# Chunk 1's x^T of a fused attention and MLP kernel: from token order and PE transposes to products in transposed order

## The chip, the cores and the metric

The kernel runs on one core of one Trainium2 chip. A core has five engines that take their instructions from queues of their own: TensorE (PE: matrix products and transposes), VectorE (DVE), ScalarE (ACT), GpSimd (POOL) and SyncE (SP, which issues most DMA transfers). They wait for each other through semaphores. SBUF is the working memory, 128 partitions wide; PSUM holds what PE writes, in banks of 512 fp32 words per partition. The metric is the device time of one execution in microseconds (us); lower is better.

## The reference: what is computed

Two blocks follow each other. The first is an attention with polynomial sketches, without softmax: 4 batches, 4 heads, 1088 tokens, head size 32, sketch size r = 8, so 64 features.

```python
def phi(x):
    a = np.einsum('rd,bhsd->bhsr', S1, x)
    b = np.einsum('rd,bhsd->bhsr', S2, x)
    return np.einsum('bhsi,bhsj->bhsij', a, b).reshape(*x.shape[:-1], r * r)
q_p, k_p = (phi(q), phi(k))
kv = np.einsum('bhsf,bhsd->bhfd', k_p, v)
z = np.sum(k_p, axis=2)
num = np.einsum('bhsf,bhfd->bhsd', q_p, kv)
den = np.einsum('bhsf,bhf->bhs', q_p, z)[..., None] + 1e-06
attn = num / den
```

The heads are laid side by side to x, 4352 tokens by 128. The second block is an MLP: `h = x @ w_in` (128 to 2048), exact GELU, `g @ w_out` (2048 to 128). w_in, w_out, S1 and S2 are 64-bit floats: they arrive as pairs of 32-bit words and are turned into fp32 on the chip.

## The kernel before, in words

**Chunks.** The tokens of each batch are cut into two chunks of 512, and what is left over (64 tokens of each batch) makes a ninth chunk. x is held transposed, x^T: 128 features on the partitions, 512 tokens along the free axis. For a chunk n and each of the 16 blocks fi of 128 hidden units, `hidden(n, fi)` is one matmul of w_in's block with xT[n], and a GELU by ACT; `project(n, fi)` adds w_out's block times that GELU to an output bank. Later chunks use a scheme with fewer products (`two_products`), which the change does not touch. `first_hidden` is hidden (n, 0) in halves of 256 tokens, so that it can begin when half of x^T is there.

**The beginning.** Chunks 0 and 1 are both of batch 0, and the MLP can't start before batch 0's kv and z are summed (`kv_first`, into kv_bank, copied by ACT to `kz[0]`). kz[0] holds, for two pairs of heads on the two halves of the partitions, kv (32 columns) and z (1 column). For chunks 0 and 1 `expand_products` makes the 64 features' two factors from q^T with 16 matmuls into two pairs of banks; `expand_copy` (ACT) copies one factor of each pair of banks to the tile A_sb, and `expand_multiply` (DVE) multiplies it with the other into qp (tile q_pT).

**x^T of chunks 0 and 1.** `numerators_by_token` makes numerator and denominator with tokens on the partitions: 32 matmuls of 33 columns. `divide` inverts the denominators and multiplies, on DVE. The result x_tok has tokens on the partitions, so PE transposes it in 128x128 pieces and ACT and DVE copy them into xT (`turn_half`, `turn_half_apart`).

**Weights.** w_in and w_out come in five pieces each (256, 256, 512, 512, 512 hidden units). The class `Rounding` turns a piece into fp32: low words and exponents on ACT, fields (exponent and mantissa fields), mantissas and signs on DVE, the product on DVE or POOL; for w_out's second piece the mantissas go through a copy by ACT (tile bits_high) and an addition on POOL (`by_pool=True`). w_in's second piece serves hidden blocks 2 and 3, w_out's second piece projections 2 and 3.

**What sets the order.** Nothing plans it: the order of the text is the order in each engine's queue, and the last lines of the kernel fix it so. The beginning is written out; from there a loop over steps t runs. Steps t = 0 to 3 are hidden (0,0) to (0,3) with w_out's first two pieces beside them; in step 3 chunk 1's numerators, division and turns stand between the first projections. Step 4 does chunk 1's first hidden, then alternates hidden and projection. PSUM has two banks each for hidden and output and two pairs of work banks.

Of the kernel before, what the change touches and what calls it, by code (L numbers as in the profile page):

```python
# [16 lines left out]
def kernel(  # L17
# [29 lines left out]
    JC = 4  # L47
    CW = JC * 128
    G = 128 // 32
    NCH = J // JC  # L50
# [26 lines left out]
    def hidden_bank():  # L77
        return hps.tile([128, CW], FP, name="h_ps")

# [149 lines left out]

    kz_first = big.tile([128, 128], FP, name="kz_first")  # L230

# [257 lines left out]
    def sketch_of_z(b, ps, at):  # L489
# [6 lines left out]
                       in1=own_r[:, None, :, None].broadcast_to([128, 2, 2, 4]))  # L496

    def repeat_first_z():

        of = kz[0].rearrange("f (r x) -> f r x", r=2)  # L500
        to = kz_first.rearrange("f (c r d) -> f c r d", c=NP, r=2)
        for c in range(NP):
            act.copy(out=to[:F, c], in_=of[c * F:(c + 1) * F, :, 0:D])
        zs = att.tile([128, 2, D], FP, name="z_cols")
        pool.tensor_copy(out=zs, in_=of[:, :, D:C].broadcast_to([128, 2, D]))
        held["zs"] = zs
# [26 lines left out]
    def expand_products(n):  # L533


        W = width[n]
        for i in range(2):
            B_of[n, i] = work_banks()
        for s in range(2):
            for g in range(G):  # L540
                for c in range(NP):
                    rows = slice(g * D, (g + 1) * D)
                    pe.matmul(B_of[n, g // 2][c * F:(c + 1) * F, g % 2, s * W // 2:(s + 1) * W // 2],  # L543
                              lhsT=Srep[rows, s].rearrange("p i j -> p (i j)"),
                              rhs=qT[n][rows, 2 * c:2 * c + 2].rearrange("p r j t -> p r (j t)"), start=True, stop=True)
        qp[n] = att.tile([128, 2, CW], FP, name="q_pT")
# [5 lines left out]
    def expand_multiply(n, i):  # L552
        W = width[n]
        a, b = (t.rearrange("f g (r x) -> f g r x", r=2) for t in (A[i][:, :, :W // 2], B_of[n, i][:, :, W // 2:W]))
        dve.tensor_mul(out=qp[n].rearrange("f r (g x) -> f g r x", g=G)[:, 2 * i:2 * i + 2], in0=a, in1=b)

# [64 lines left out]
    def attend_products(n, banks=None):  # L621
# [7 lines left out]
        for i in range(m):  # L629
            for s in range(2):  # L630
                rows, b = slice(s * 64, (s + 1) * 64), batch_of(n, s, i)
                for h in range(H):
                    pe.matmul(banks[h * D:(h + 1) * D, s, i * N:(i + 1) * N],  # L633
                              lhsT=(kz[b] if b else kz_first)[rows, h * D:(h + 1) * D],
                              rhs=f[rows, h // 2, i, :, h % 2], start=True, stop=True)
        numerators_in[n] = banks

    def take_x(n):
# [4 lines left out]
        to = to.rearrange("p (s x) -> p s x", s=2) if m == 1 else to.rearrange("p (s t i) -> p s i t", s=2, i=m)  # L643
        act.copy(out=to, in_=banks[:, :, :W // 2] if m == 1 else banks[:, :, :W // 2].rearrange("p s (i t) -> p s i t", i=m))  # L644

    x_tok = {}
# [95 lines left out]
    T = {}  # L742
    HW = CW // 2
    NPAIR = NF // 2
# [184 lines left out]
    kz_of, kv_of = (x.rearrange("f (r x) -> f r x", r=2)[:, :, :C] for x in (kz[0], kv_bank[:, :128]))  # L929
    act.copy(out=kz_of, in_=kv_of)  # L930
    w_in[0].mantissas()
    w_in[0].signs()
    w_in[0].product(pool)
    load_w_out(0, gated=True)
    load_rest()
    w_out = [Rounding(w, beside=b) for w, b in zip(w_out_sb[:2], w_in)]
    by_act(**late[0])
    w_in[1].low_words()
    parts = [range(2), range(2, JC)]
    nd = [[hidden_bank(), hidden_bank()], [out_bank(), out_bank()]]  # L940
    for banks, tokens in zip(nd, parts):
        numerators_by_token(0, banks, tokens)
    den = denominators(nd[1])
    expand_products(1)
    divide(0, nd[0], parts[0], by_head_pair=True)
    w_in[1].exponent_fields()
    w_in[1].exponents()
    divide(0, nd[1], parts[1], by_head_pair=True, den=den)
    turn_half(0, 0, hidden_bank(), by_act)
    w_in[1].mantissa_fields()  # L950
    turn_half_apart(0, 1, [out_bank(), out_bank()])
    w_in[1].mantissas()
    w_in[1].signs()
    w_in[1].product()
    for half in range(2):
        first_hidden(0, half)
    for i in range(2):
        expand_copy(1, i)
    for i in range(2):
# [204 lines left out]
    for t in range(len(steps) + LAG):  # L1164
        if t < 4:
# [7 lines left out]
            if t == 2:  # L1173
                w_out[1].low_words()
            if t == 3:
                banks = work_banks()
                numerators_by_token(1, halves(banks), range(JC))
                w_out[1].mantissas(by_pool=True)
                w_out[1].exponents()
                divide(1, banks, range(JC), by_head_pair=False)  # L1180
                w_out[1].signs()
                w_out[1].product()
                project(0, 0)
                project(0, 1, cols=slice(0, 256))
                turn_half(1, 0, work_bank(), by_act)
                project(0, 1, cols=slice(256, 512))
                turn_half(1, 1, work_bank(), by_dve)
            continue
        if t == 4:
            first_hidden(1, 0)  # L1190
            for f, *a in products[t]:
                f(*a)
            first_hidden(1, 1)
        for n in drains[t]:
# [60 lines left out]
```

## Time and profile before

| | us |
|---|---|
| median of 3 runs | 259.5 (259.48 to 259.85) |
| span of the profiled execution, first to last instruction | 258.0 |
| PE busy | 253.9 (98% of the span) |
| DVE / ACT / POOL busy | 151.0 / 115.5 / 163.5 |
| numerators of chunk 1 on PE (L656) | 19.11 to 20.25 |
| hidden (1,1) begins on PE (L721) | 24.24 |

The profile gives no total of its own for the profiled execution beside its span; the span is 1.5 us under the median of the runs. A line of a timeline or a group names source line, engine, operation, output<-input by the program's tile names, and a count. PE works as two records per fp32 matmul. Busy time says little on an engine off the critical path; what counts here is the order of events between 12 and 25 us and what each instruction waited for. Lines in the profile are those of the kernel before.

### The profile page before, as it was taken

What the parts mean: (1) busy time and instruction counts of PE and PEld (TensorE: products, weight loads), DVE (VectorE), ACT (ScalarE), POOL (GpSimd) and SP (SyncE); (2) the same over time, 40 slices, a digit from 0 to 9 for tenths busy, and PEclk for the clock granted to TensorE, in tenths of its full rate; (3) what the DMA queues carried; (4) which work ended last, traced back from release to release, by engine and by line L of the source; (5) the groups of instructions that cost most, each with busy time, mean ns of one, the idle gap of its engine ahead of it and who ended that gap; (6) DMA issues with size and microseconds to landing.
All of it is one profiled execution on the core that took longest, in us unless ns stands there. A gap on an engine that the chain in (4) does not pass through costs nothing.

```text
span 258.0 us, 5769 instructions
## 1 busy us (share of the span) xinstructions
PE 253.9 (98%) x2335; PEld 136.1 (53%) x2335; DVE 151.0 (59%) x312; ACT 115.5 (45%) x224; POOL 163.5 (63%) x173
## 2 busy tenths in 40 slices
PE   8999999999999999999999999999999999999995
PEld 7856444345444545544444455455444444445794
DVE  2786888969699997590187986399307000700330
ACT  4685777443626332443335332533444334433442
POOL 3403006799968788487758775787758777877300
PEclk9999999999999999999999999999999999999999
DMA  6469848721000101102000002000200200020020
GB/s 199 144 185 374 188 95 217 213 76 14 3 0 12 31 1 21 23 6 37 3 0 3 0 9 38 0 1 3 41 3 4 39 0 1 7 36 0 3 41 20
DMA packets 29594, 13.48 MB, mean 52 GB/s; under 512 B 21888, under 2 KB 27776, under 8 KB 29568
## 3 DMA queue, kind: packets, MB, share of 16 engines
q1 hardware_dynamic: 29392, 13.05, 20.3%
q8 instruction: 18, 0.29, 0.5%
q10 hardware_dynamic: 176, 0.07, 0.1%
q14 instruction: 8, 0.07, 0.1%
HBM read 10.88 MB, written 2.23 MB: 51 GB/s over the span
## 4 chain that ended last, share of the span: by engine, by line
PE 98%; DVE 1%; issue 0%; ACT 0%; DVEq 0%
PE h_ps L721 45%; PE o_ps L807 33%; PE o_ps L858 5%; PE w_ps L855 3%; PE w_ps L437 1%; PE w_ps L890 1%; PE w_ps L578 1%; PE w_ps L633 1%; PE o_ps L426 1%; PE h_ps L737 1%; PE w_ps L978 1%; PE w_ps L656 0%; PE w_ps L543 0%; DVE x_tok L679 0%; PE h_ps L333 0%; PE w_ps L333 0%
## 5 line engine op out<-in xcount | busy, mean ns | idle before, releaser
L721 PE MATMUL h_ps<-xT,w_in 128*64 128x512 f32 (+3 forms) x514 | 136.9, 576 | 0.0
L728 ACT ACTIVATE block<-h_ps 128x512 f32<-128x512 f32 (+1 forms) x128 | 73.0, 571 | 117.3 <-PE h_ps L721 115.3
L721 PEld LDWEIGHTS h_ps<-xT,w_in 128*64 128x64 f32 (+1 forms) x514 | 41.9, 143 | 30.4 <-issue 11.6
L807 PE MATMUL o_ps<-block,w_out 128*64 128x256 f32 x224 | 57.5, 379 | 0.0
L772 POOL TENSOR_TENSOR bits_low<-block 128x512 f32<-128x512 f32 x28 | 35.9, 1281 | 27.8 <-ACT block L728 27.8
L807 PEld LDWEIGHTS o_ps<-block,w_out 128*64 128x64 f32 x224 | 30.5, 137 | 38.0 <-issue 27.5
L773 POOL TENSOR_TENSOR bits_a<-block 128x512 f32<-128x512 f32 x28 | 35.7, 1277 | 12.0 <-ACT block L728 11.9
L822 DVE COPY sums<-o_ps 64x256 f32<-64x256 f32 x8 | 3.3, 416 | 60.6 <-PE o_ps L807 60.6
L774 POOL TENSOR_TENSOR bits_e<-bits_a,block 128x512 f32<-128x512 f32 x28 | 36.0, 1286 | 2.2
L775 POOL TENSOR_TENSOR bits_m<-block,bits_e 128x512 f32<-128x512 f32 x28 | 35.8, 1279 | 2.2
L807 PE MATMUL o_ps<-bits_low,small 128*64 128x256 f32 x112 | 28.8, 380 | 0.0
L807 PE MATMUL o_ps<-bits_a,small 128*64 128x256 f32 x112 | 28.8, 380 | 0.0
L807 PE MATMUL o_ps<-block,small 128*64 128x256 f32 x112 | 28.8, 379 | 0.0
L807 PE MATMUL o_ps<-bits_m,w_out 128*64 128x256 f32 x112 | 28.8, 380 | 0.0
L807 PEld LDWEIGHTS o_ps<-block,small 128*64 128x64 f32 x112 | 15.2, 137 | 17.9 <-issue 10.8
L807 PE MATMUL o_ps<-bits_e,small 128*64 128x256 f32 x112 | 17.1, 383 | 0.0
L858 PE MATMUL o_ps<-g,w_out 128*128 128x512 f32 (+1 forms) x34 | 16.5, 572 | 0.0
L807 PEld LDWEIGHTS o_ps<-bits_m,w_out 128*64 128x64 f32 x112 | 15.4, 137 | 0.0
L807 PEld LDWEIGHTS o_ps<-bits_a,small 128*64 128x64 f32 x112 | 15.2, 137 | 0.0
L807 PEld LDWEIGHTS o_ps<-bits_low,small 128*64 128x64 f32 x112 | 15.2, 137 | 0.0
L590 DVE STREAM_TRANSPOSE w_ps<-w_ps 128x512 f32<-128x512 f32 (+1 forms) x7 | 4.8, 687 | 17.1 <-ACT xT L644 12.7
L807 PEld LDWEIGHTS o_ps<-bits_e,small 128*64 128x64 f32 x112 | 7.7, 137 | 10.6 <-issue 8.8
(194 smaller groups left out, 305.1 us busy)
## 6 DMA issues: line engine op xcount, KB each, us to landing
block<-in_moe_w_in_dram SPq DMA_DIRECT2D x3, 512.0 KB, 8.4
block<-in_moe_w_out_dram SPq DMA_DIRECT2D x3, 512.0 KB, 12.1
k<-in_k_dram SPq DMA_DIRECT2D x12, 128.0 KB, 3.1
v<-in_v_dram SPq DMA_DIRECT2D x12, 128.0 KB, 3.4
q<-in_q_dram SPq DMA_DIRECT2D x24, 64.0 KB, 2.4
out_dram<-oT SPq DMA_DIRECT2D x21, 64.0 KB, 2.2
k<-in_k_dram SPq DMA_DIRECT2D x2, 256.0 KB, 2.8
q<-in_q_dram SPq DMA_DIRECT2D x2, 256.0 KB, 3.9
```

The costliest lines, as they stand in the source:

```text
L426: pe.matmul(ps[c * F:(c + 1) * F, r * 2 * D:r * 2 * D + C], lhsT=flat(k_p[0, r][:, t, c * 4 + ch * 2 + one]), rhs=v_aug[r][:, c, i, :C], s ...
L590: dve.transpose(out=tok, in_=ps[:, :, :H2])
L721: pe.matmul(ps[rows, :W], lhsT=w[:, rows], rhs=xT[n][:, :W], start=True, stop=True)
L728: act.activation(out=g_of[n, fi][:, :W], in_=ps[:, :W], func=ACT.Gelu)
L772: pool.tensor_sub(out=s[3], in0=a11, in1=a21)
L773: pool.tensor_add(out=s[1], in0=a21, in1=a22)
L774: pool.tensor_sub(out=s[2], in0=s[1], in1=a11)
L775: pool.tensor_sub(out=s[4], in0=a12, in1=s[2])
L807: pe.matmul(acc[n][bank][half * 64:(half + 1) * 64, col:col + HW], lhsT=fixed, rhs=moving, start=opens and e == 0 and name in "4715", stop ...
L822: dve.tensor_copy(out=N[lo, 0, one], in_=a0[lo, one])
L855: pe.matmul(o_of[n][i][:, :128], lhsT=g[:, i * 128:(i + 1) * 128], rhs=w_tile(w_out_sb, fi), start=first, stop=final)
L858: pe.matmul(o_of[n][:, cols], lhsT=w_tile(w_out_sb, fi), rhs=g[:, cols], start=first, stop=final)
```

## The change

x^T of chunk 1 is made without turning x back by PE. ACT spreads kz[0] into `kz_both`, which holds all four heads' kv and z on each half of the partitions (four copies of 64x66, right behind the copy of kz[0]); POOL repeats z 32 times per head (`z_wide`). The features of chunk 1 are laid so that each half of the partitions holds all heads of half of the tokens. `ratio_products` then makes, with 16 matmuls of 32 output rows and 256 columns, the denominators repeated over 32 rows and the numerators, both already transposed. `ratio_inverse` turns the repeated denominators in 32x32 blocks on DVE, takes one column of each, adds 1e-6 and inverts; `ratio` turns them back, repeated, and multiplies the numerators into xT[1], in two halves.

In the order: the products stand in step 2, ahead of the hidden block of step 3; the inverse and the multiplications stand beside w_out's second piece in step 3; projections (0,0) and (0,1) are no longer interleaved with turns, and chunk 1's first hidden now follows projection (0,2). w_in's second piece: both fields on DVE ahead of chunk 0's divisions, exponents on ACT ahead of the copies of chunk 0's x^T, mantissas and signs behind the divisions, the product on POOL. The first A_sb copy of chunk 1 moves on ACT ahead of these exponents, the second behind the copies of chunk 0's x^T. `kz_first`, which the ninth chunk used, is replaced by kz_both.

```diff
--- before.py
+++ after.py
@@ -46,6 +46,7 @@
     REM = S - MAIN
     JC = 4
     CW = JC * 128
+    HW = CW // 2
     G = 128 // 32
     NCH = J // JC
     C = D + 1
@@ -227,7 +228,8 @@
 
     kz = [big.tile([128, 128], FP, name=f"kz{b}") for b in range(B)]
 
-    kz_first = big.tile([128, 128], FP, name="kz_first")
+    kz_both = big.tile([128, H, 2 * D], FP, name="kz_both")
+    z_wide = big.tile([128, H, D], FP, name="z_wide")
 
     ones = big.tile([128, D], FP, name="ones")
 
@@ -495,12 +497,19 @@
         dve.tensor_mul(out=S_abc[b][:, :, :, 4:8], in0=c.rearrange("p (i f) -> p i f", i=2)[:, :, None].broadcast_to([128, 2, 2, 4]),
                        in1=own_r[:, None, :, None].broadcast_to([128, 2, 2, 4]))
 
+    def spread_first_kv():
+
+        of = kz[0].rearrange("f (r x) -> f r x", r=2)
+        for s in range(2):
+            for c in range(NP):
+                act.copy(out=kz_both[s * F:(s + 1) * F, 2 * c:2 * c + 2, :C], in_=of[c * F:(c + 1) * F, :, :C])
+
+    def spread_first_z():
+        pool.tensor_copy(out=z_wide, in_=kz_both[:, :, D:C].broadcast_to([128, H, D]))
+
     def repeat_first_z():
 
         of = kz[0].rearrange("f (r x) -> f r x", r=2)
-        to = kz_first.rearrange("f (c r d) -> f c r d", c=NP, r=2)
-        for c in range(NP):
-            act.copy(out=to[:F, c], in_=of[c * F:(c + 1) * F, :, 0:D])
         zs = att.tile([128, 2, D], FP, name="z_cols")
         pool.tensor_copy(out=zs, in_=of[:, :, D:C].broadcast_to([128, 2, D]))
         held["zs"] = zs
@@ -542,7 +551,8 @@
                     rows = slice(g * D, (g + 1) * D)
                     pe.matmul(B_of[n, g // 2][c * F:(c + 1) * F, g % 2, s * W // 2:(s + 1) * W // 2],
                               lhsT=Srep[rows, s].rearrange("p i j -> p (i j)"),
-                              rhs=qT[n][rows, 2 * c:2 * c + 2].rearrange("p r j t -> p r (j t)"), start=True, stop=True)
+                              rhs=(qT[n][rows, :, 2 * c:2 * c + 2] if n else qT[n][rows, 2 * c:2 * c + 2])
+                              .rearrange("p r j t -> p r (j t)"), start=True, stop=True)
         qp[n] = att.tile([128, 2, CW], FP, name="q_pT")
 
     def expand_copy(n, i):
@@ -551,6 +561,10 @@
 
     def expand_multiply(n, i):
         W = width[n]
+        if n:
+            dve.tensor_mul(out=qp[n].rearrange("f r (g x) -> f (r g) x", g=2)[:, 2 * i:2 * i + 2],
+                           in0=A[i][:, :, :W // 2], in1=B_of[n, i][:, :, W // 2:W])
+            return
         a, b = (t.rearrange("f g (r x) -> f g r x", r=2) for t in (A[i][:, :, :W // 2], B_of[n, i][:, :, W // 2:W]))
         dve.tensor_mul(out=qp[n].rearrange("f r (g x) -> f g r x", g=G)[:, 2 * i:2 * i + 2], in0=a, in1=b)
 
@@ -631,7 +645,7 @@
                 rows, b = slice(s * 64, (s + 1) * 64), batch_of(n, s, i)
                 for h in range(H):
                     pe.matmul(banks[h * D:(h + 1) * D, s, i * N:(i + 1) * N],
-                              lhsT=(kz[b] if b else kz_first)[rows, h * D:(h + 1) * D],
+                              lhsT=kz[b][rows, h * D:(h + 1) * D] if b else kz_both[rows, h, :D],
                               rhs=f[rows, h // 2, i, :, h % 2], start=True, stop=True)
         numerators_in[n] = banks
 
@@ -642,6 +656,36 @@
         to = xT[n][:, :W]
         to = to.rearrange("p (s x) -> p s x", s=2) if m == 1 else to.rearrange("p (s t i) -> p s i t", s=2, i=m)
         act.copy(out=to, in_=banks[:, :, :W // 2] if m == 1 else banks[:, :, :W // 2].rearrange("p s (i t) -> p s i t", i=m))
+
+    def ratio_products(n, banks):
+
+        f = qp[n].rearrange("f r (g h t) -> f h (r g) t", g=2, h=H)
+        for at, w in ((HW, lambda rows, h: z_wide[rows, h]), (0, lambda rows, h: kz_both[rows, h, :D])):
+            for s in range(2):
+                rows = slice(s * F, (s + 1) * F)
+                for h in range(H):
+                    pe.matmul(banks[h * D:(h + 1) * D, s, at:at + HW], lhsT=w(rows, h), rhs=f[rows, h], start=True, stop=True)
+
+    def ratio_inverse(banks):
+
+        turned = att.tile([128, 2 * CW], FP, name="q_f", bufs=1)
+        dve.transpose(out=turned[:, :CW].rearrange("p (g s x) -> p s g x", g=G, s=2),
+                      in_=banks[:, :, HW:].rearrange("p s (g x) -> p s g x", g=G))
+        den = att.tile([128, NP, JC * 2], FP, name="den_tok").rearrange("p c k -> p (c k)")
+        dve.tensor_scalar(out=den, in0=turned[:, :CW].rearrange("p (k x) -> p k x", x=D)[:, :, 0], scalar1=1e-6, scalar2=None,
+                          op0=AX.add)
+        dve.reciprocal(out=den, in_=den)
+        return den, turned[:, CW:]
+
+    def ratio(n, banks, den, wide):
+
+        xT[n] = att.tile([128, CW], FP, name="xT", bufs=3)
+        for i in range(2):
+            cols = slice(i * HW, (i + 1) * HW)
+            dve.transpose(out=wide[:, cols], in_=den[:, i * 8:(i + 1) * 8, None].broadcast_to([128, 8, D]))
+            by = lambda t: t.rearrange("p (g s x) -> p s g x", g=2, s=2)
+            dve.tensor_mul(out=by(xT[n][:, cols]), in0=banks[:, :, i * 128:(i + 1) * 128].rearrange("p s (g x) -> p s g x", g=2),
+                           in1=by(wide[:, cols]))
 
     x_tok = {}
 
@@ -740,7 +784,6 @@
 
     blocks, sums, acc = {}, {}, {}
     T = {}
-    HW = CW // 2
     NPAIR = NF // 2
 
     PLACE = {"1": (0, 0, 0), "2": (0, 0, HW), "3": (1, 0, 0), "5": (1, 0, HW),
@@ -928,34 +971,35 @@
     query_turn(1, lambda **a: late.append(a))
     kz_of, kv_of = (x.rearrange("f (r x) -> f r x", r=2)[:, :, :C] for x in (kz[0], kv_bank[:, :128]))
     act.copy(out=kz_of, in_=kv_of)
+    spread_first_kv()
     w_in[0].mantissas()
     w_in[0].signs()
     w_in[0].product(pool)
     load_w_out(0, gated=True)
     load_rest()
+    spread_first_z()
     w_out = [Rounding(w, beside=b) for w, b in zip(w_out_sb[:2], w_in)]
     by_act(**late[0])
     w_in[1].low_words()
+    w_in[1].fields()
     parts = [range(2), range(2, JC)]
     nd = [[hidden_bank(), hidden_bank()], [out_bank(), out_bank()]]
     for banks, tokens in zip(nd, parts):
         numerators_by_token(0, banks, tokens)
     den = denominators(nd[1])
     expand_products(1)
+    expand_copy(1, 0)
+    w_in[1].exponents()
     divide(0, nd[0], parts[0], by_head_pair=True)
-    w_in[1].exponent_fields()
-    w_in[1].exponents()
     divide(0, nd[1], parts[1], by_head_pair=True, den=den)
-    turn_half(0, 0, hidden_bank(), by_act)
-    w_in[1].mantissa_fields()
-    turn_half_apart(0, 1, [out_bank(), out_bank()])
     w_in[1].mantissas()
     w_in[1].signs()
-    w_in[1].product()
+    w_in[1].product(pool)
+    turn_half(0, 0, hidden_bank(), by_act)
+    turn_half_apart(0, 1, [out_bank(), out_bank()])
     for half in range(2):
         first_hidden(0, half)
-    for i in range(2):
-        expand_copy(1, i)
+    expand_copy(1, 1)
     for i in range(2):
         expand_multiply(1, i)
     w_out[0].fields()
@@ -1172,24 +1216,23 @@
                 w_out[1].fields()
             if t == 2:
                 w_out[1].low_words()
+            if t == 2:
+                banks = work_banks()
+                ratio_products(1, banks)
             if t == 3:
-                banks = work_banks()
-                numerators_by_token(1, halves(banks), range(JC))
                 w_out[1].mantissas(by_pool=True)
                 w_out[1].exponents()
-                divide(1, banks, range(JC), by_head_pair=False)
+                inverse = ratio_inverse(banks)
                 w_out[1].signs()
                 w_out[1].product()
+                ratio(1, banks, *inverse)
                 project(0, 0)
-                project(0, 1, cols=slice(0, 256))
-                turn_half(1, 0, work_bank(), by_act)
-                project(0, 1, cols=slice(256, 512))
-                turn_half(1, 1, work_bank(), by_dve)
+                project(0, 1)
             continue
         if t == 4:
-            first_hidden(1, 0)
             for f, *a in products[t]:
                 f(*a)
+            first_hidden(1, 0)
             first_hidden(1, 1)
         for n in drains[t]:
             drain(n)
```

## The prediction

> **What bounds the kernel now.** I read the page first, for the bound.
>
> ```profile
> PE 253.9 (98%) x2335; PEld 136.1 (53%) x2335; DVE 151.0 (59%) x312; ACT 115.5 (45%) x224; POOL 163.5 (63%) x173
> PEclk9999999999999999999999999999999999999999
> PE 98%; DVE 1%; issue 0%; ACT 0%; DVEq 0%
> ```
>
> TensorE (PE) is busy throughout at full clock, and the chain that ended last is PE from 15.04 us to the end: there the list of waits has no PE wait over the 0.2 us before L694. So whatever PE gains or loses before about 25 us moves the end by as much. The change lies between 12 and 25 us; hence the timeline there, PE first (start, duration, engine, line).
>
> ```profile
> 7.71 1.12 PE L543 MATMUL w_ps<-qT,Srep 32*64 32x256 f32 x32
> 13.34 1.12 PE L543 MATMUL w_ps<-qT,Srep 32*64 32x256 f32 x32
> 14.39 0.44 PE L702 MATMUL h_ps<-ident,x_tok 128*128 128x128 f32 x2
> 15.04 0.41 PE L694 MATMUL o_ps<-ident,x_tok 128*128 128x128 f32 x2 [0.21 <-DVE x_tok L679]
> 15.38 1.13 PE L737 MATMUL h_ps<-xT,w_in 128*128 128x128 f32 x8
> 16.35 2.84 PE L721 MATMUL h_ps<-xT,w_in 128*128 128x512 f32 x6
> 19.11 1.14 PE L656 MATMUL w_ps<-kz,q_pT 64*64 64x33 f32 x64
> 20.18 1.56 PE L858 MATMUL o_ps<-g,w_out 128*128 128x512 f32 x4
> 24.24 1.02 PE L721 MATMUL h_ps<-xT,w_in 128*128 128x512 f32 x2
> 68.99 0.64 PE L633 MATMUL w_ps<-q_pT,kz 64*32 64x256 f32 x16
> ```
>
> A matmul is two records, and a 512-column one takes 0.86 us of PE (pairs start that far apart). At 24.24 starts hidden(1,1), by which projections (0,0) to (0,2), hidden (0,0) to (0,3) and chunk 1's first hidden are done; after the change the same work is done when hidden(1,1) starts. I measure the change by that start. Then ScalarE (ACT), which has the copies:
>
> ```profile
> 7.38 0.33 ACT L398 COPY a_t<-o_ps 128x64 f32<-128x64 f32 x2 [0.43 <-PE o_ps L382]
> 8.87 1.07 ACT L550 COPY A_sb<-w_ps 128x512 f32<-128x512 f32 x2 [0.60 <-PE w_ps L543]
> 12.38 0.59 ACT L937 COPY qT<-w_ps 128x512 f32<-128x512 f32 x1 [0.34 <-PE w_ps L333]
> 12.86 0.44 ACT L260 ACTIVATE bits_low<-small 128x256 f32<-128x256 uint32 x1
> 14.28 0.51 ACT L279 ACTIVATE bits_r<-bits_e,below 128x256 uint32<-128x256 uint32 x1 [0.58 <-DVE bits_e L268]
> 14.86 0.37 ACT L703 COPY xT<-h_ps 128x256 f32<-128x256 f32 x1
> 19.62 0.58 ACT L728 ACTIVATE g<-h_ps 128x512 f32<-128x512 f32 x1
> 20.27 0.42 ACT L284 ACTIVATE bits_high<-bits_a 128x256 f32<-128x256 uint32 x1
> 20.60 0.49 ACT L279 ACTIVATE bits_r<-bits_e,below 128x256 uint32<-128x256 uint32 x1
> 22.13 0.45 DVE L297 TENSOR_TENSOR w_out<-bits_m,bits_e 128x256 f32<-128x256 f32 x1
> 85.87 0.49 ACT L503 COPY kz_first<-kz 64x64 f32<-64x64 f32 x2
> ```
>
> Three things to see. The A_sb copy of chunk 0 (8.87) began 0.04 us after the last record of its products (7.71+1.12 = 8.83), although it needs only the first of the two bank pairs. Two small copies out of PSUM (7.38) overlap: 0.33 us for two of 0.22, so 0.11 apart. Two SBUF-to-SBUF copies that change partition halves (85.87) do not: 0.49 for two, 0.24 apart. And bits_high, the first step of w_out's second piece, follows gelu (0,3) at 19.62 in ACT's queue.
>
> **The change, part by part** (waits as the two built programs order them; engines take their queues in order).
>
> *1. Four spread copies ahead of the qT copy.* They follow the kz copy (11.84 to 12.04) on ACT, each 64x66 SBUF to SBUF, alternating partition halves. Unknown price: 0.11 apart (L398) or 0.24 (L503). I take 0.24: same engine, same memories, same alternation. Then they run from 12.07 to 13.05, and the qT copy that took 12.38 to 12.97 takes 13.06 to 13.65. Chunk 1's products (L543, 13.34) wait for it: hand-over 0.06, start 13.71, late by 0.37. At 0.11 apart qT ends at 13.10 and nothing is late. Ends: 0 and 0.37.
>
> *2. A_sb copy and exponents now stand ahead of chunk 0's xT copy on ACT.* By the 8.87 row the A_sb copy starts 0.04 after the last product: 13.71+1.12+0.04 = 14.87. The next ACT starts follow 0.48 (half of the L550 pair's start distance) and 0.42 later (18.40 to 18.81 in the same view): exponents 15.35, xT copy 15.77, to 16.14 at 0.37. first_hidden starts 0.06 later, 16.20, where L737 started at 15.38: **+0.82** with step 1's 0.37 inside. Its bounds: 0.45 if step 1 costs nothing; 0.22 less if the A_sb copy waited only for the third quarter of the products. The DVE step taken out between the divisions (L268, 0.20) would have let PE transposes start 0.20 earlier; ACT's copy is later, so it is worth 0.
>
> *3. w_in's second piece.* Its fields go before the first division: DVE idles 0.54 before 12.99 and two such steps start 0.20 apart, so they fit; its load landed long before 12.46, as ACT read it freely at 12.86. Mantissas and signs follow the divisions, signs end at 16.32 (exponents end 15.86, plus 0.04 and 0.42); the product on POOL takes 0.73 (the first piece's), 16.40 to 17.13. hidden(0,2) needs it at 17.21+0.82 = 18.03: hidden by 0.9, and z_wide ahead of it on POOL too (0.23 for 128x64 to 0.61 for 128x512, from about 13.3). That cover is gone only if signs slip past 17.2. No transfer is moved; SP's queue is as before, and the gating memsets on POOL still come before z_wide.
>
> *4. PE work.* Removed: the 32 numerators of L656 (19.02, when hidden(0,3)'s last record gives way, to 20.18: 1.16, and 0.10 of exposed weights behind), four transposes (0.11 each, 0.44) and 0.08 of weights: 1.78. Added: 16 matmuls of the form of L633, eight of which take 0.43; with the 0.10 and 0.14 that this timeline shows on entering and leaving such tiles, and 0.09 of exposed weights behind: 1.21 (0.88 of it the matmuls). Net **-0.57**. If only four of the eight tiles ran at once, 0.88 more.
>
> *5. hidden(0,3) moves behind the products, and gelu (0,3) with it; bits_high still stands behind that gelu.* hidden(0,2) starts at 18.03, takes 0.95 (its first record pair is 0.52 apart, as now), the products 1.12 to hidden(0,3) at 20.11, whose last record ends at 21.22. gelu (0,3) at 21.26 (now 19.62); bits_high 0.48 later, 21.73; exponents 22.06 to 22.55. DVE: signs 22.59 to 23.01, product (L297, 0.45, 0.10 after) 23.11 to 23.56, where it ended at 22.58. POOL's share (0.73 from 22.23) ends before. project (0,2) needs those weights: 0.15 later (as L694 after x_tok), 23.71. PE gets there at 21.06+2x0.86 = 22.78. New wait **+0.93**; queued behind it are chunk 1's first hidden and hidden(1,1).
>
> *6. Chunk 1's x^T.* Its first turn and inverse (0.73 for a 128x512 turn out of PSUM, 0.17, 0.25, as rows L590, L673, L674) run from 20.82 to 22.04, inside DVE's wait for the exponents: worth nothing while that wait stands. Behind the w_out product come two pairs of a 128x256 turn (0.40, the L528 row of that size) and a multiplication (0.42, L413): 23.45, 23.89 to 24.31, 24.23, 24.67 to 25.09. First half ready before PE's 24.57; the second at 25.15, PE is there at 25.00: **+0.15**. hidden(1,1) then starts at 25.58.
>
> Sum: 0.82 - 0.57 + 0.93 + 0.15 = **+1.33 us**. The page's span of 258.0 becomes 259.3; the median of the runs is 259.5, 1.5 above the span, which I take as unchanged: 260.8. Nothing gives it back: PE has no wait after 25 us that a later PE would shorten. w_in's third piece keeps about 1 us of room (now done at 28.2, needed at 29.4; both move).
>
> **The rivals.**
> *The spread copies overlap.* For it the L398 pair; against it the L503 pair. Then step 2 costs 0.45, the rest of the chain is 0.37 earlier: +0.96, 260.5. [...]
>
> *w_out's second piece comes sooner.* Were bits_high and exponents run before gelu (0,3), in the 0.8 us that ACT idles there, the product would wait for DVE alone: inverse done 22.04, signs 22.0 to 22.4, product 22.5 to 22.95, project (0,2) at 23.10, a wait of 0.32 for 0.93; the second half's 0.15 stays. +0.72, 260.2. Against: the queue's order. With overlapping copies as well +0.35, 259.85: no measurable change.
>
> *Faster: a waiting instruction does not hold those behind it.* Then exponents and chunk 0's xT copy pass the A_sb copy, bits_high passes gelu (0,3), and the turns pass the w_out product; only PE's work counts, with the 0.20 taken off DVE: -0.57 - 0.20 = -0.77, 258.7. It decides if ACT begins the xT copy by 14.86, before its A_sb copy. Against, in this trace: ACT idles 2.14 us before a gelu at 24.50 and only then runs a bits_low (25.00) whose piece DVE had read at 22.99.
>
> *The products share the array worse* (their moving operand is in runs of 64 with strides): 0.88 more, 261.7. Against: L633's operand is strided too.
>
> **How the numbers follow.** Forecast 0.56, overlapping copies 0.16, w_out sooner 0.08, worse products 0.05: slower, 0.85. Both of the milder ones together 0.09: same. Passing instructions 0.06: faster. A difference under 0.2% (0.5 us) is about what a measurement of this kernel can't tell from none; the three runs spread over 0.37. The range goes from 259.8 (the two milder ones together) to 261.3 (forecast with some 0.25 us of error at either of two hand-overs); it leaves out the faster case and the worse products, 0.11, and tails.
>
> **What would show it.** After: the spread copies 0.24 apart and the qT copy near 13.06; the A_sb copy near 14.87; first_hidden near 16.2; a PE wait of 0.9 us before the third projection, ended by DVE's w_out product; hidden(1,1) near 25.6. Copies 0.11 apart take off 0.37. It is wrong if ACT takes the xT copy before 15, or if bits_high ends before gelu (0,3) begins, or if PE waits again later for work that now comes closer (w_in's third piece past 30 us).

## The result, and the profile after

The changed kernel takes 261.34 us (median of five runs, 261.05 to 261.76), the kernel before in the same session 259.48: a ratio of 1.0076, 95% interval 1.0059 to 1.0093. It is slower, as forecast, by 1.9 to 2.0 us where 1.33 was forecast; 261.34 lies just past the end of the range given (261.3).

On the page of the changed kernel (busy time by engine, granted clock by slices of the span, the chain that ended last), nothing of the bound has changed:

```profile
PE 252.8 (98%) x2297; PEld 133.7 (52%) x2297; DVE 152.9 (59%) x311; ACT 115.3 (44%) x225; POOL 164.7 (64%) x175
PEclk9999999999999999999999999999999999999999
PE 93%; ACT 2%; DMA 2%; DVE 1%; issue 0%; SPq 0%; DVEq 0%
```

PE is busy 1.1 us less than before (253.9; busy time takes in the modelled ends of the records, so the sum further down goes by starts), and yet it ends later: the time went into waits. The list of PE's waits between 11 and 26 us names them (waiting instruction, releaser, total us, times, longest):

```profile
PE o_ps L901 <- DVE w_out L299: 1.0, 1, 1.0
PE h_ps L781 <- ACT xT L747: 0.4, 1, 0.4
PE w_ps L552 <- ACT qT L982: 0.3, 1, 0.3
PE o_ps L738 <- DVE x_tok L723: 0.2, 1, 0.2
```

The last of these stood in the kernel before as well (0.21); the other three are new. The timeline of PE after (start, duration, line) shows where they lie:

```profile
12.96 1.12 PE L552 MATMUL w_ps<-qT,Srep 32*64 32x256 f32 x32 [0.34 <-ACT qT L982]
15.52 1.13 PE L781 MATMUL h_ps<-xT,w_in 128*128 128x128 f32 x8 [0.42 <-ACT xT L747]
16.48 2.04 PE L765 MATMUL h_ps<-xT,w_in 128*128 128x512 f32 x4
18.45 0.66 PE L667 MATMUL w_ps<-q_pT,z_wide 64*32 64x256 f32 x16
18.91 0.64 PE L667 MATMUL w_ps<-q_pT,kz_both 64*32 64x256 f32 x16
19.48 1.13 PE L765 MATMUL h_ps<-xT,w_in 128*128 128x512 f32 x2
20.44 1.88 PE L901 MATMUL o_ps<-g,w_out 128*128 128x512 f32 x4
23.37 1.10 PE L901 MATMUL o_ps<-g,w_out 128*128 128x512 f32 x2 [1.05 <-DVE w_out L299]
24.30 1.30 PE L781 MATMUL h_ps<-xT,w_in 128*128 128x256 f32 x4
25.44 0.59 PE L765 MATMUL h_ps<-xT,w_in 128*128 128x512 f32 x1
```

hidden(1,1), the mark used in the prediction, starts at 25.44. That this stands so near the forecast's 25.6 is chance, because these absolute times can't be compared with those of before directly. Executions of one and the same kernel differ in how late the work around the change begins: the copy of kz[0] on ACT, the last event that the change leaves in place, began at 11.84 us in the profile of before and at 11.66 when that kernel was profiled again, at 11.04 and 11.49 in two profiles of the changed one. The profiles show what goes with it: PE's first transposes of 128 columns start 0.21 us apart in some executions and 0.11 in others. In the six of the twelve profiles of this document where they are still 0.21 apart at 5.9 us, the copy begins at 11.65 to 11.84; in the six where they have gone over to 0.11 by then, at 10.98 to 11.54. What follows that copy repeats to 0.01 us. So from here on "kz + x" is x us after the start of that copy:

| | before | after |
|---|---|---|
| chunk 1's products begin | kz + 1.50 | kz + 1.92 |
| chunk 0's first hidden | 3.54 | 4.47 |
| hidden(0,2) | 5.37 | 6.38 |
| project (0,0) | 8.34 | 9.39 |
| hidden(1,1) | 12.40 | 14.39 |
| the last copy of the output (ACT, tile oT) ends | 243.32 | 245.34 |

The whole difference, 2.0 us, has arisen by hidden(1,1), and the 230.9 us behind it are the same in both. ACT's timeline after shows the first half of it:

```profile
11.04 0.20 ACT L973 COPY kz<-o_ps 128x66 f32<-128x66 f32 x1
11.27 1.03 ACT L505 COPY kz_both<-kz 64x66 f32<-64x66 f32 x4
12.32 0.58 ACT L982 COPY qT<-w_ps 128x512 f32<-128x512 f32 x1
14.12 0.58 ACT L560 COPY A_sb<-w_ps 128x512 f32<-128x512 f32 x1 [0.62 <-PE w_ps L552]
14.60 0.51 ACT L281 ACTIVATE bits_r<-bits_e,below 128x256 uint32<-128x256 uint32 x1
15.01 0.36 ACT L747 COPY xT<-h_ps 128x256 f32<-128x256 f32 x1
20.64 0.60 ACT L772 ACTIVATE g<-h_ps 128x512 f32<-128x512 f32 x1 [0.96 <-PE h_ps L765]
21.13 0.41 ACT L286 ACTIVATE bits_high<-bits_a 128x256 f32<-128x256 uint32 x1
21.44 0.50 ACT L281 ACTIVATE bits_r<-bits_e,below 128x256 uint32<-128x256 uint32 x1
```

The four spread copies take 1.03 us and don't overlap; the qT copy follows them; the A_sb copy and the exponents hold up the x^T copy, which begins at 15.01 although its transposes were done by 14.46 (14.02 + 0.44). Below, gelu (0,3) at 20.64 and bits_high only behind it. The same timeline for DVE and POOL shows what follows:

```profile
21.68 0.73 POOL L287 TENSOR_TENSOR bits_m<-bits_high,bits_low 128x256 f32<-128x256 f32 x1 [5.30 <-ACT bits_high L286]
21.97 0.72 DVE L294 SCALAR_TENSOR_TENSOR bits_e<-small,bits_r 128x256 uint32<-128x256 uint32 x1 [0.67 <-ACT bits_r L281]
22.80 0.43 DVE L299 TENSOR_TENSOR w_out<-bits_m,bits_e 128x256 f32<-128x256 f32 x1
23.61 0.42 DVE L687 TENSOR_TENSOR xT<-w_ps,q_f 128x256 f32<-128x256 f32 x1
```

The signs take 0.72 us, and POOL's addition runs beside them. The product ends at 23.22 and lets project (0,2) go at 23.37. In the kernel before, the signs came after POOL's addition and took 0.41 (timelines of POOL and DVE before):

```profile
20.77 0.73 POOL L285 TENSOR_TENSOR bits_m<-bits_high,bits_low 128x256 f32<-128x256 f32 x1 [7.43 <-ACT bits_high L284]
20.81 0.89 DVE L679 TENSOR_TENSOR x_tok<-w_ps,den_tok 128x128 f32<-128x128 f32 x4
21.62 0.41 DVE L292 SCALAR_TENSOR_TENSOR bits_e<-small,bits_r 128x256 uint32<-128x256 uint32 x1
```

What stood beside the addition there were the four multiplications of x_tok, which read PSUM. They took 0.28 to 0.29 us each, as they do elsewhere with POOL idle, so these rows didn't show that the addition could cost DVE anything.

### The profile page after: what moved, and what is told of

The parts are those of the page before. It is cut to its first block, busy times and chain, and to the rows that moved or that the text cites. A ratio compares the mean times of both kernels' runs of the same rounds, so it can differ in the third digit from the quotient of the medians.

```text
span 259.3 us, 5693 instructions
## 1 busy us (share of the span) xinstructions
PE 252.8 (98%) x2297; PEld 133.7 (52%) x2297; DVE 152.9 (59%) x311; ACT 115.3 (44%) x225; POOL 164.7 (64%) x175
## 4 chain that ended last, share of the span: by engine, by line
PE 93%; ACT 2%; DMA 2%; DVE 1%; issue 0%; SPq 0%; DVEq 0%
PE h_ps L765 45%; PE o_ps L850 33%; PE o_ps L901 5%; PE w_ps L898 3%; DMA q<-in_q_dram 2%; PE w_ps L439 1%; PE w_ps L592 1%; PE w_ps L647 1%; PE w_ps L552 1%; PE h_ps L781 1%; PE w_ps L1022 1%; ACT bits_r L281 1%; DVE q_pT L569 0%; ACT A_sb L560 0%; PE w_ps L667 0%; ACT kz_both L505 0%
## 5 line engine op out<-in xcount | busy, mean ns | idle before, releaser
L901 PE MATMUL o_ps<-g,w_out 128*128 128x512 f32 x32 | 16.3, 597 | 1.0 <-DVE w_out L299 1.0
L772 ACT ACTIVATE g<-h_ps 128x512 f32<-128x512 f32 x16 | 9.5, 596 | 10.2 <-PE h_ps L765 5.7
```

Source lines behind the costliest of these rows:

```text
L772: act.activation(out=g_of[n, fi][:, :W], in_=ps[:, :W], func=ACT.Gelu)
L901: pe.matmul(o_of[n][:, cols], lhsT=w_tile(w_out_sb, fi), rhs=g[:, cols], start=first, stop=final)
```

## The experiments

Each starts from the changed kernel unless its text names another, and shows its edit; lines left out are marked with three dots. All times of a group are set against runs of the kernel before on the same chip (medians 259.24, 259.27 and 259.30 us in three groups).

### Step 1, the spread copies: taken off ACT

```diff
 def spread_first_kv():
-                act.copy(out=kz_both[...], in_=of[...])
+                pool.tensor_copy(out=kz_both[...], in_=of[...])
...
     act.copy(out=kz_of, in_=kv_of)
-    spread_first_kv()
...
     load_rest()
+    spread_first_kv()
     spread_first_z()
```

> The four spread copies go from ScalarE to POOL, behind the gating memsets; nothing else moves. Theory (ScalarE's queue delays chunk 0's x^T): the qT copy starts when its transposes end, some 0.7 us sooner, chunk 1's products 0.35 to 0.4 us sooner, and all behind them as much: 260.9 to 261.0, where the changed kernel has 261.3. Rival (the copies are covered, the delay is the A_sb copy's alone): the products start as late as before, 261.3.

Measured: 261.25 us, ratio 1.0073 (1.0055 to 1.0092), no better than the change, and the 260.9 to 261.0 expected didn't come. The qT copy went from kz + 1.28 to kz + 0.54, where before has it, but the products began at kz + 1.97. PE's timeline says why:

```profile
11.57 0.55 PE L700 MATMUL h_ps<-kz,q_pT 64*64 64x33 f32 x23
12.38 0.32 PE L700 MATMUL h_ps<-kz,q_pT 64*64 64x33 f32 x9 [0.27 <-issue]
13.10 1.12 PE L552 MATMUL w_ps<-qT,Srep 32*64 32x256 f32 x32
```

In the middle of chunk 0's numerators PE stopped, and the profile shows nothing that it waited for ("issue"). Between the last start ahead of it and the next start lie 0.49 us in place of less than 0.05, about what the edit had won. This run settles nothing about step 1; the next one does.

### Step 1 alone, in the kernel before

```diff
...
     act.copy(out=kz_of, in_=kv_of)
+    spread_first_kv()
     w_in[0].mantissas()
```

The function and the tile kz_both are those of the change. Nothing reads what these copies write.

> The kernel before with step 1 alone: four copies of kz's halves, 64 x 66 each, on ACT between the kz copy and the qT copy; what they write is not read. Theory of step 1: they lie 0.26 apart, the qT copy goes from kz + 0.5 to kz + 1.27, chunk 1's products from kz + 1.50 to kz + 1.9, and as nothing behind them waits for anything but them, hidden(1,1) from kz + 12.40 to kz + 12.8: 259.3 becomes 259.7 us. Rival (the chain through chunk 0's division is the one that decides, and the products have slack): products as late as that, but first_hidden still at kz + 3.54, and 259.3 us.

Measured: 259.62 us, ratio 1.0013 (1.0003 to 1.0022). Timelines of ACT and PE:

```profile
11.21 0.20 ACT L938 COPY kz<-o_ps 128x66 f32<-128x66 f32 x1
11.44 1.03 ACT L504 COPY kz_both<-kz 64x66 f32<-64x66 f32 x4
12.49 0.58 ACT L946 COPY qT<-w_ps 128x512 f32<-128x512 f32 x1
13.13 1.12 PE L551 MATMUL w_ps<-qT,Srep 32*64 32x256 f32 x32 [0.26 <-ACT qT L946]
15.18 1.13 PE L745 MATMUL h_ps<-xT,w_in 128*128 128x128 f32 x8
24.04 1.02 PE L729 MATMUL h_ps<-xT,w_in 128*128 128x512 f32 x2
```

Products at kz + 1.92, first hidden at kz + 3.97, hidden(1,1) at kz + 12.83, against 1.50, 3.54 and 12.41: the 0.42 of step 1 is passed on whole. The rival, slack behind the products, is out. In the medians the four copies cost 0.35 us (0.1 to 0.6 by the interval).

### Step 2, the A_sb copy ahead of the x^T copy: put behind it

```diff
     expand_products(1)
-    expand_copy(1, 0)
     w_in[1].exponents()
...
         first_hidden(0, half)
+    expand_copy(1, 0)
     expand_copy(1, 1)
```

> The first A_sb copy of chunk 1 goes behind the copies of chunk 0's x^T on ScalarE; the exponents stay ahead of them. Theory: the x^T copy starts right behind PE's transposes, 0.5 us sooner against the products, and first_hidden and all behind it 0.5 us sooner: 260.8. Rival (PE waits there for VectorE's divisions or the weights anyway): 261.3.

Measured: first hidden at kz + 3.96 (4.47 in the change), hidden(1,1) at kz + 13.88 (14.39); 261.14 us, ratio 1.0072 (1.0054 to 1.0091). PE's list of waits has lost the x^T copy:

```profile
PE o_ps L901 <- DVE w_out L299: 1.0, 1, 1.0
PE w_ps L552 <- ACT qT L982: 0.3, 1, 0.3
```

So this order costs 0.51 us in the trace. The medians show 0.2 of it, where 0.5 was expected; what is missing is within their spread.

### Step 5, gelu (0,3) ahead of bits_high: the order turned round

```diff
             if t == 2:
                 banks = work_banks()
                 ratio_products(1, banks)
-            if t == 3:
                 w_out[1].mantissas(by_pool=True)
                 w_out[1].exponents()
+            if t == 3:
                 inverse = ratio_inverse(banks)
```

> bits_high and the exponents of w_out's second piece go ahead of gelu (0,3) on ScalarE. Theory (project (0,2) waits for w_out's second piece because its first step stands behind that gelu): the product of w_out ends 0.6 to 1.0 us sooner, PE's wait before project (0,2) falls from 1.2 to between 0.2 and 0.6 us: 260.3 to 260.7. Rival (VectorE's own work is the bound there): at most 0.2 us, 261.1 to 261.3.

Measured: project (0,2) at kz + 11.74 (12.32 in the change), hidden(1,1) at kz + 13.81; 260.91 us, ratio 1.0058 (1.0037 to 1.0080). That is 0.58 us off a wait of 1.21, so the queue's order was about half of it. The expectation was narrowly missed: 0.63 of wait is left where 0.2 to 0.6 was expected, and 260.91 lies between the theory and its rival. POOL's addition now comes earlier, and its neighbour on DVE is another (timelines of DVE and POOL):

```profile
21.41 0.72 POOL L287 TENSOR_TENSOR bits_m<-bits_high,bits_low 128x256 f32<-128x256 f32 x1 [4.40 <-ACT bits_high L286]
21.48 0.69 DVE L675 TENSOR_SCALAR den_tok<-q_f 128x16 f32<-128x16 f32 x1
22.38 0.36 DVE L294 SCALAR_TENSOR_TENSOR bits_e<-small,bits_r 128x256 uint32<-128x256 uint32 x1
```

L675, an addition on 16 columns, takes 0.69 us in place of 0.18 and ends 0.04 after POOL's addition does; the signs, now alone, take 0.36.

### Step 5, w_out's mantissas without POOL

```diff
             if t == 3:
-                w_out[1].mantissas(by_pool=True)
                 w_out[1].exponents()
                 inverse = ratio_inverse(banks)
+                w_out[1].mantissas()
                 w_out[1].signs()
```

> The mantissas of w_out's second piece are made by VectorE, as for the first piece, and not by a copy on ScalarE and an addition on POOL; the order is otherwise kept. In the changed kernel the signs step took 0.72 us beside POOL's addition, where it takes 0.42 elsewhere. If POOL's addition slows it: signs 0.42, product of w_out 0.6 us sooner, 260.7. If the signs step is slow for another reason: signs 0.72 again, product 0.3 us sooner, 261.0.

Measured: project (0,2) at kz + 11.65, hidden(1,1) at kz + 13.72, 0.67 earlier than in the change; 260.71 us, ratio 1.0056 (1.0037 to 1.0074). From DVE's timeline:

```profile
21.73 0.36 DVE L289 SCALAR_TENSOR_TENSOR bits_m<-bits_a,bits_low 128x256 f32<-128x256 uint32 x1
22.16 0.42 DVE L294 SCALAR_TENSOR_TENSOR bits_e<-small,bits_r 128x256 uint32<-128x256 uint32 x1
```

The signs are back at 0.42 us with POOL idle beside them, so POOL's addition is what stretched them. The stretched step follows that addition through three kernels: signs in the change, L675 in the run above, none here. Not all of the 0.67 is POOL's: 0.30 is the shorter signs, and another 0.30 comes from the exponents, which start earlier because ACT no longer has the bits_high copy ahead of them.

### Three repairs at once

POOL's spread copies, the later A_sb copy and the mantissas on DVE, all in one kernel (the three diffs above).

> The changed kernel with three of the edits at once: spread copies on POOL, chunk 0's x^T copies ahead of the first A_sb copy on ACT, and the mantissas of w_out's second piece on VectorE. Alone they moved hidden(1,1), counted from the kz copy, from 14.39 to 14.49, 13.88 and 13.72 us. Theory (the three waits lie one behind the other on one chain, so gains add): 14.39 - 0.51 - 0.67 and nothing from the first = 13.2, so 261.3 - 1.2 = 260.1 us if the stall of 0.45 us among chunk 0's numerators comes again, and 12.8 and 259.7 if it does not and step 1's 0.42 is won. Rival (the waits share one cause further back, VectorE's own work, and the second gain eats the first): 13.7 and 260.7, as with the third alone.

Measured: 259.87 us, ratio 1.0015 (0.9996 to 1.0033). Products at kz + 1.50, first hidden 3.59, project (0,2) 10.82, hidden(1,1) 12.89. PE didn't stop among the numerators, so the 0.42 of step 1 was won here; the sum of the three (0.42 + 0.51 + 0.67 = 1.60) gives 12.79, and 12.89 was measured. The waits lie one behind the other and add up, to 0.1. Two waits are left on PE; the second stood in the kernel before too, at 0.2:

```profile
PE o_ps L901 <- DVE w_out L299: 0.4, 1, 0.4
PE o_ps L738 <- DVE x_tok L723: 0.3, 1, 0.3
```

### The two kernels again

> The kernel before again, for one more profiled execution. What is asked is where its clock of work stands: in the profile shown before the prediction the copy of k^T v (the kz copy on ACT, L930) began 11.84 us from the start and the span was 258.0; in the five profiles of the changed kernel and its variants that copy began at 11.04 to 11.68. Theory: the start varies from execution to execution by several tenths in either kernel, and the change does not touch it; then this look has the kz copy anywhere between 11.0 and 11.9, the products of chunk 1 begin 1.50 after it and hidden(1,1) 12.40 after it, as in the first profile, and span less that start stays at 246.1 to 246.3. Rival: the change itself moves the start (by 0.2 to 0.8 us earlier); then this look has the kz copy at 11.8 again.

Measured: 259.65 us, kz copy at 11.66, hidden(1,1) at kz + 12.41, end at kz + 243.33.

> The changed kernel again, on the same chip and against the same runs of the kernel before as the rearranged ones. Theory: what the change costs is the 2.0 us that its work from the kz copy to the end is longer (245.34 against 243.33), whatever the start does: a ratio of 1.0070 to 1.0085, 261.0 to 261.5 us, with the kz copy anywhere from 11.0 to 11.9. Rival: the first five runs, whose median of 261.34 lay above all but one of the variants' medians, were slow by their chip; then 260.9 us or less.

Measured: 261.43 us, ratio 1.0078 (1.0064 to 1.0092), kz copy at 11.49, hidden(1,1) at kz + 14.39, end at kz + 245.33. The difference is 2.00 us in the traces and 2.1 in the medians. In each of these executions the time is the start of the kz copy, plus what follows, plus 4.66 to 4.67 us. DVE's timeline in this second profile of the change shows the fields of w_in's second piece, with POOL's product of the first piece beside them (12.19 to 12.92):

```profile
12.02 0.29 DVE L270 TENSOR_SCALAR bits_e<-small 128x256 uint32<-128x256 uint32 x1
12.22 0.87 DVE L275 TENSOR_SCALAR bits_a<-small 128x256 uint32<-128x256 uint32 x1
```

The second, which took 0.29 in the kernel before (14.81), takes 0.87.

### A rearrangement without the new waits

The change with POOL's spread copies and the later A_sb copy, and:

```diff
+            if t == 0:
+                w_out[0].low_words()
             hidden(0, t)
-            if t == 1:
-                w_out[0].low_words()
+            if t == 0:
                 w_out[0].exponents()
                 w_out[0].finish()
+            if t == 1:
                 w_out[1].fields()
-            if t == 2:
                 w_out[1].low_words()
-            if t == 2:
+            if t == 1:
                 banks = work_banks()
                 ratio_products(1, banks)
-            if t == 3:
-                w_out[1].mantissas(by_pool=True)
+            if t == 2:
                 w_out[1].exponents()
                 inverse = ratio_inverse(banks)
-                w_out[1].signs()
-                w_out[1].product()
+                w_out[1].finish()
+            if t == 3:
                 ratio(1, banks, *inverse)
```

> The changed kernel, arranged so that none of the new waits should stand: spread copies on POOL; chunk 0's x^T copies ahead of the A_sb copies; chunk 1's ratio products one step earlier, between hidden(0,1) and hidden(0,2), where PE waits for gelu(0,0) anyway; w_out's first low words ahead of gelu(0,0); its second piece finished on VectorE right behind the inverse, before the halves of x^T. Theory (the change costs time only by those waits, and its PE work is 0.57 us less): hidden(1,1) at kz + 12.0 to 12.4 against 12.40 of before and 14.39 of the changed kernel, so 258.9 to 259.4 us. Rival (VectorE has become the bound of this stage: its fields, signs, products, turns and divisions there come to some 6.5 us without a gap): hidden(1,1) at kz + 13 or later, 259.9 us or more.

Measured: 259.51 us, ratio 1.0001 (0.9992 to 1.0010), hidden(1,1) at kz + 12.34. The new wait for w_out is gone, and the kernel can't be told from the one before; hidden(1,1) lies in the range expected, the time 0.1 above it. The rival, DVE as the bound of this stage, is out. One new wait appeared:

```profile
17.70 0.67 PE L667 MATMUL w_ps<-q_pT,z_wide 64*32 64x256 f32 x16 [0.31 <-POOL S_abc L489]
```

The releaser named is a copy on POOL that these products don't read; the tile from POOL that they do read, z_wide, was done at 14.69. What they also read is chunk 1's features, and DVE ended those at 17.55. The next run changes only that.

### The A_sb copy back ahead of the x^T copy

```diff
     w_in[1].exponents()
+    expand_copy(1, 0)
     divide(0, nd[0], parts[0], by_head_pair=True)
...
         first_hidden(0, half)
-    expand_copy(1, 0)
     expand_copy(1, 1)
```

> As the rearranged kernel before it, with one order changed: the first A_sb copy goes back ahead of chunk 0's x^T copies on ACT, while the exponents that stood between them stay ahead of both. In the rearranged kernel PE stood still for 0.47 us ahead of the ratio products, waiting for chunk 1's features, whose second half VectorE ended at 17.55. Theory (that wait came from the A_sb copy alone): it ends right behind the products, so the x^T copy is only 0.1 later, the features are ready 0.35 to 0.5 earlier, and hidden(1,1) comes at kz + 11.9 to 12.1 instead of 12.34: about 259.0 to 259.1 us, 0.25 to 0.35 under the kernel before. Rival (VectorE's queue behind the features sets the two halves of x^T anyway, and the x^T copy is as late as in the changed kernel): hidden(1,1) at kz + 12.3 or later, 259.4 us or more.

Measured: 259.23 us, ratio 0.9993 (0.9983 to 1.0003), hidden(1,1) at kz + 12.09. PE's timeline runs through:

```profile
16.34 1.02 PE L765 MATMUL h_ps<-xT,w_in 128*128 128x512 f32 x2
17.30 0.66 PE L667 MATMUL w_ps<-q_pT,z_wide 64*32 64x256 f32 x16
18.32 1.98 PE L765 MATMUL h_ps<-xT,w_in 128*128 128x512 f32 x4
20.14 2.74 PE L901 MATMUL o_ps<-g,w_out 128*128 128x512 f32 x6
22.71 1.20 PE L781 MATMUL h_ps<-xT,w_in 128*128 128x256 f32 x4
```

The features are done at 16.94, kz + 5.28 where the run above had 5.74, and the wait ahead of the products is gone, so it was for them. By the traces this version is 0.31 us shorter than the kernel before (end at kz + 243.01 against 243.32), as expected; by the runs the two can't be told apart, the interval includes 1.

## What the prediction had right, and the step that failed

All six steps took place where they were put, and the change is slower by the waits that were named. Their sizes were wrong: the sum was 1.33 where the trace has 1.99, and 261.34 lies past the range. The step that failed is step 5, the new wait for w_out: 0.93 was forecast and 1.21 measured, because POOL's addition was priced at nothing for the DVE step beside it. The other 0.38 of the difference lies in smaller terms, all to the same side: 0.13 in step 6, 0.11 in steps 1 and 2, 0.08 in a hand-over that no step had, 0.06 in step 4. Term by term, the first two from the table above, the rest worked out below:

| term of the sum | forecast | measured |
|---|---|---|
| steps 1 and 2, first hidden | +0.82 | +0.93 (4.47 - 3.54) |
| wait of hidden(0,2) for gelu (0,0) | 0 | +0.08 (6.38 - 5.37, less 0.93) |
| step 4, PE work | -0.57 | -0.51 (what is left) |
| step 5, new wait for w_out | +0.93 | +1.21 |
| step 6, second half of x^T | +0.15 | +0.28 |
| sum | +1.33 | +1.99 |

*Step 1* took the price of the copies that change partition halves, and that held: 0.26 apart at 0.25 each, for 0.24. The rival with overlapping copies is out: the two copies out of PSUM that spoke for it (0.22 each, 0.11 apart) overlap in the kernel before, these four don't. So are the others: ACT took the x^T copy (15.01) behind the A_sb copy (14.12) and bits_high (21.13) behind gelu (0,3) (20.64), as queued, and the ratio products took 1.02 us from their start to hidden(0,3), where 1.12 was forecast. What keeps the four copies apart stays open: bits_high and the exponents behind it, from SBUF to SBUF too, overlap by 0.10 (21.13 + 0.41 against 21.44), and neither the size nor the change of partition halves was varied alone.

*Step 2* had the order right to the hundredth: A_sb copy 1.16 after the products' start, exponents 0.48 after that, x^T copy 0.41 after those. It was short by two hand-overs, and by 0.05 for the copies of step 1. The 0.06 taken from copy to PE is 0.05 for the products behind the qT copy (12.91 to 12.96), but 0.14 for the first hidden behind the x^T copy (15.37 to 15.52). The kernel before has 0.14 in the same place (15.24 to 15.38), so the forecast's own rows had the better price. It is 0.14 again for hidden(0,2) behind gelu (0,0) (17.28 to 17.43), which no step had. In the kernel before, hidden(0,2) started 0.06 after the end of that GELU (17.15 to 17.21). There its weights came from DVE and now from POOL; whether that makes the difference was not tested. The range allowed for 0.25 of error at hand-overs; it did not allow for the two terms below as well.

*Step 3* was right about the product: POOL ended it at 16.38, and it was needed at 17.43. It was wrong about the fields, which were to fit into DVE's idle 0.54. Beside POOL's product of the first piece one of them took 0.65 us in the first profile of the change and 0.87 in the second, where the two took 0.28 and 0.29 before. In the first profile their load also landed only at kz + 0.93, so chunk 0's divisions began at kz + 1.82 there and at kz + 1.53 in the second profile, against 1.15 before. This cost nothing here: the first hidden came at kz + 4.47 in both, because ACT's queue held the x^T copy longer still.

*Step 4* was right to 0.06, as the remainder; in the last rearrangement, PE goes from first hidden to hidden(1,1) in 8.37 us where before took 8.86, with 0.17 of wait still inside.

*Step 5* is the term that failed most. Projection (0,1)'s last record starts at 21.73 and its pace is 0.43, so PE was there at 22.16 and went on at 23.37: 1.21. Its signs were put at 0.42, with POOL's share noted only as ending in time. POOL's addition was in time and still cost 0.30, by slowing the step beside it. From the start of gelu (0,3) to project (0,2) the prediction had 2.45 us, the trace has 2.73, and the signs alone make that difference. With the mantissas on DVE the 0.30 went away. What the traces show is which steps were hit: the signs, with both inputs in SBUF, went from 0.42 to 0.72; the multiplications of x_tok, with one input in PSUM, took 0.28 to 0.29 each beside the addition and with POOL idle. In the run with the turned order DVE's step, begun 0.07 after POOL's, ended 0.04 after it. In the change not all of the step was held up until POOL's end: the signs ended 0.28 after the addition, and alone they take 0.42. By what means POOL slows them was not shown.

*Step 6* was 0.13 short. The four passes of chunk 1's first hidden start 0.22, 0.38, 0.32 and 0.22 apart where 0.215 is the pace without a wait (1.14 - 0.86 = 0.28). The wait for the second half of x^T itself is 0.17, close to the 0.15 forecast. The other 0.10 comes behind it: the pass with which PE goes on is followed by the next after 0.32. The kernel before shows the same after a wait for x^T (22.45, then 22.74), and the forecast left it out.

The base was no error: 260.8 is the median of before plus 1.33, and with 1.99 it would have been 261.5, against 261.34 and 261.43.

## What to carry to other kernels

A change that takes work off the bounding engine can be paid for in the queues of the others: here 0.5 us less on PE came with 2.5 us of new delays (0.93, 0.08, 1.21 and 0.28), most of it from what stood ahead of a needed step in the queues of ACT and DVE, 0.30 from a DVE step that POOL slowed. Another order in those queues, with one step moved to POOL and one off it, gave it all back. When a step of POOL is said to end in time, look also at what DVE runs beside it, and price that one too; here it counted for signs (0.42 to 0.72 us) and fields (0.29 to between 0.65 and 0.87), whose inputs lie in SBUF, and not for the multiplications into x_tok and q_pT that read PSUM (0.28 to 0.29 and 0.68, beside POOL or not). And where the beginning of a kernel varies between executions, compare traces from an event that the change leaves alone: single hundredths could be read that way (hidden(1,1) of the kernel before at kz + 12.40 and 12.41), while the medians of that kernel went from 259.24 to 259.48.

## What the runs showed of the hardware that was not expected

- Some DVE steps beside a POOL addition or product of 0.73 us were stretched, and ended 0.04 to 0.28 us after POOL's: the signs from 0.42 to 0.72, the addition on 16 columns from 0.18 to 0.69, and a field step of w_in from 0.29 to 0.65 in the first profile of the change and to between 0.84 and 0.87 in its second and in all seven kernels made from it. Others were not: the multiplications into q_pT, with one input in PSUM, took 0.68 beside POOL's product in the change and 0.68 before, and a 128x512 transpose out of SBUF (L912 of the change) takes 0.71 beside POOL (at 81.41) and alone (at 247.97).
- The hand-over to PE has no single price: in the changed kernel 0.05 us from the qT copy, 0.14 from the x^T copy and from gelu (0,0), 0.15 from w_out's product. What makes the difference was not tested.
- PE stopped for 0.27 us of idle time among 64 small matmuls in one profile and showed no such stop in three others with the same copies on POOL. It remains unexplained. In that profile the last transfer on the instruction queue (q8) ahead of the stop began at kz - 1.13, in the eleven others at kz - 2.41 to kz - 1.46; whether the two belong together was not tested.
